# Logit matmuls in batches of eight, four logit banks, smaller PSUM and staging pools, and half-1 products written into the first phase

## The chip, the cores and the metric

The kernel runs on one core of a Trainium2 chip. The metric is device time in microseconds (us) of that core, taken over several executions; lower is better. A run here is slow when it lies over 1.5% above the fastest run of its kernel. The granted clock is the share of TensorE's full clock that the profile records. Engines are named as the profile names them: PE is TensorE (matmul), PEld its weight loads, DVE VectorE, ACT ScalarE, POOL GpSimd, SP SyncE (here it only issues DMAs). "L527" is line 527 of the kernel. "Compiled order" is the order in which the compiler puts the instructions on each engine; it can be read from a build, without a chip, and it isn't always the order of the source.

## The reference

Two independent blocks whose outputs are joined along the last axis. Part A is a dilated sliding-window attention (16 heads of 28, 8 taps, dilation 2); part B is a diagonal complex state-space layer ("S5").

```python
# A: x [1,2048,448] bf16
q, k, v = split(x @ wqkv)                       # 16 heads, Dh = 28
idx = pos[:, None] - 2 * arange(8)[None, :]     # W = 8 taps, dilation 2
logits = einsum("bhsd,bhswd->bhsw", q, k[idx]) * Dh**-0.5   # masked where idx < 0
o = einsum("bhsw,bhswd->bhsd", softmax(logits), v[idx])
a = o.reshape(B, S, D) @ wo
# B: h_t = Lam_bar * h_{t-1} + B_bar x_t ;  y = 2 Re(C h) + x * Dskip
out = concatenate([a, b], axis=-1)              # [1,2048,896] bf16
```

## The kernel before

Part B's recurrence (the "S5 chain") runs on VectorE. Its output needs 16 "y tiles": 12 matmuls of 128x448 each into one PSUM bank, a ScalarE cast into a staging buffer `yb`, and a store.

Part A's logits are made in two halves of the sequence. For every tap w and quarter mt of the heads, VectorE multiplies q by the shifted k (the tile `pr`, 32 of them a half, 64 in all), and TensorE sums over the head dimension with an indicator matrix into the logit banks `lg`, two banks a half, one per chunk `ci` of 512 columns. Softmax works on chunk after chunk of 512. After it come 56 products `td` of attention and gathered v, reductions of them into a PSUM bank `ot`, its eviction `oT`, and 16 output-projection tiles that use the same staging buffers `yb`. The core, with cuts marked:

```python
    ps_mm = pool("ps_mm", bufs=3, space=PSUM)     # projections, softmax      (shortened)
    ps_lg = pool("ps_lg", bufs=2, space=PSUM)     # logits: one half at a time
    ps_y  = pool("ps_y",  bufs=2, space=PSUM)
    ps_ot = pool("ps_ot", bufs=1, space=PSUM)
    ap: bufs=6 (pr)      yo: bufs=3 (yb)
    # ...
            p0 = A.products(0)
            for tl in range(HB // 128):
                B.y_slice(1, tl)                  # ... 12 matmuls, then:
                #   yb = yo.tile(...); nc.scalar.copy(yb[:], ps[:])
                #   nc.sync.dma_start(outv[...], yb[:])
                for em in p0[4 * tl:4 * tl + 4]:
                    em()
    # ... products(hf), one em per (w, mt):
                    pr = ap_.tile([112, HF], BF16, name="pr")
                    nc.vector.tensor_tensor(pr[:], qT[...], kT[...], op=ALU.mult)
                    for ci in range(HF // CH):
                        nc.tensor.matmul(lg[ci][32 * g:32 * g + 32, :], lhsT=IndZ[:, o0:o0 + 32],
                                         rhs=pr[:, ci * CH:(ci + 1) * CH], ...,
                                         tile_position=(0, 32 * g))      # g = w // 2
    # ... late():
            for gi in range(4):
                load_vwg(gi)                      # gathered v (vwG), 2 MB each, on SyncE's queue
            p1 = products(1)
            sm01 = zip_stages(softmax(0), softmax(1))
            left = interleave(sm01, p1, 3)        # 3 products after each softmax stage
```

## Time and profile before

| | before |
|---|---|
| median of 4 runs (range) | 284.79 us (284.36 to 285.24) |
| profiled span | 283.5 us |
| VectorE / TensorE busy | 75% / 71% |

The windows of before follow. A line is one stretch of time (from:to, its length), then busy us of each engine with the number of instructions, then the granted TensorE clock as a share of full speed, the DMA share and GB/s.

```profile
core 0: us, PE busy (x) PEld busy (x) DVE busy (x) ACT busy (x) POOL busy (x), PEclk, DMA share, GB/s
146.50:166.00 19.50, 19.30 (x66) 3.43 (x66) 19.50 (x33) 0.00 (x0) 0.00 (x0) 0.87 0.36 119
166.80:193.20 26.40, 25.21 (x133) 12.78 (x132) 1.98 (x5) 5.89 (x12) 0.00 (x0) 1.00 0.79 280
...
243.60:262.60 19.00, 12.60 (x66) 2.23 (x65) 19.00 (x32) 5.27 (x9) 0.00 (x0) 0.50 0.56 212
...
262.60:283.50 20.90, 17.27 (x70) 5.93 (x70) 0.01 (x1) 9.75 (x19) 0.00 (x0) 0.88 0.27 88
```

Four stages can be read there. From 146 VectorE is full with products and TensorE keeps up. From 167 TensorE is full with y tiles and VectorE almost empty. The last 19 us of the td products have a full VectorE and TensorE at half clock. In the tail VectorE has ended and TensorE works at the output projection.

VectorE's timeline around the y stage (start, duration, instruction group, and in brackets the idle time ahead of it and what ended it):

```profile
start us, us, engine line op out<-in xcount [idle before <-releaser]
...
145.76 22.97 DVE L527 TENSOR_TENSOR pr<-qT,kT 112x1024 bf16<-112x1024 bf16 x38
193.15 1.28 DVE L584 TENSOR_TENSOR m<-lg,t 64x512 f32<-64x512 f32 x2 [24.42 <-ACT t L580]
```

So 38 products run without a gap, 0.604 us each, and then VectorE waits 24.4 us for the softmax's first copy, which stands behind the y tiles.

From the waits (engine, line, what it waited for: us in total, times, longest):

```profile
...
DVE m L584 <- ACT t L580: 24.4, 1, 24.4
...
PE ot L637 <- ACT oT L642: 8.0, 9, 2.5
...
ACT yb L407 <- DMA out_dram<-yb: 6.9, 2, 4.5
```

The first line is the wait of the timeline again. The second is TensorE waiting nine times for its one `ot` bank to be evicted (copied out to SBUF). The third is a cast that waits for a staging buffer, because the store of its old content hasn't landed.

ScalarE in the tail of before:

```profile
start us, us, engine line op out<-in xcount [idle before <-releaser]
...
276.38 0.58 ACT L642 CAST oT<-ot 64x512 bf16<-64x512 f32 x1 [0.93 <-PE ot L637]
276.86 1.13 ACT L655 CAST yb<-y 128x448 bf16<-128x448 f32 x2
278.44 0.53 ACT L655 CAST yb<-y 128x448 bf16<-128x448 f32 x1 [0.45 <-PE y L652]
279.19 0.53 ACT L655 CAST yb<-y 128x448 bf16<-128x448 f32 x1 [0.23 <-PE y L652]
280.02 0.53 ACT L655 CAST yb<-y 128x448 bf16<-128x448 f32 x1 [0.29 <-PE y L652]
```

The last casts come singly, some 0.8 us apart, as TensorE finishes its tiles.

### The profile page before, as it was taken

The page shows a single profiled execution, that of the slowest core. Times are in us where ns is not written, and L with a number is a line of the kernel's source. Part 1 is how long each engine was busy: PE and PEld are TensorE (multiplying, and loading weights), DVE is VectorE, ACT ScalarE, POOL GpSimd, SP SyncE. Part 2 cuts the span into 40 slices and gives each one's busy share as a digit, 9 for nine tenths or more (in the row PEclk, how much of TensorE's full clock was granted, in tenths as well). Part 3 has the DMA queues.
Part 4 walks back from the last instruction along what each step waited for, and adds up shares of the span by engine and source line. Part 5 has one row for each costly group of instructions (what it writes and reads, how often), then busy time and mean ns, then how long its engine had stood idle before and what let it go on. Part 6 is the DMA issues. An engine that isn't in the chain of part 4 may idle for free.

```text
span 283.5 us, 2644 instructions
## 1 busy us (share of the span) xinstructions
PE 201.1 (71%) x836; PEld 76.5 (27%) x836; DVE 213.6 (75%) x324; ACT 126.2 (44%) x199; POOL 32.3 (11%) x58
## 2 busy tenths in 40 slices
PE   0067164298969896959539999986986635666994
PEld 0012032044535453525201135541211101111231
DVE  4907999989999999999999980005899629999000
ACT  4019319399675877466500002217603490222454
POOL 8928143000040000000000000002000000000000
PEclk9997759589988999999958999998799555555699
DMA  5999821113279998850027008992000005980132
GB/s 125 215 194 232 219 65 31 49 51 98 66 239 335 321 322 323 322 230 32 1 50 279 0 2 291 354 333 89 2 1 0 0 0 168 415 299 7 49 118 92
DMA packets 40109, 42.68 MB, mean 151 GB/s; under 512 B 26140, under 2 KB 32480, under 8 KB 40096
## 3 DMA queue, kind: packets, MB, share of 16 engines
q1 hardware_dynamic: 37984, 35.18, 40.3%
q0 software_dynamic: 2112, 7.34, 7.7%
q8 instruction: 6, 0.10, 0.1%
q14 instruction: 7, 0.06, 0.1%
HBM read 30.97 MB, written 20.20 MB: 180 GB/s over the span
## 4 chain that ended last, share of the span: by engine, by line
DVE 53%; PE 23%; DMA 7%; ACT 7%; issue 6%; SPq 4%; POOL 0%; DVEq 0%; ACTq 0%; POOLq 0%
PE lg L534 7%; DVE gre L378 6%; DVE gim L379 6%; DVE td L627 6%; DMA out_dram<-yb 5%; PE y L652 5%; PE ot L637 5%; DVE pr L527 4%; DVE wt L318 3%; DVE wt L320 2%; SPq L84 2%; DVE vre L365 2%; DVE tA L366 2%; DVE vre L367 2%; DVE tB L371 2%
## 5 line engine op out<-in xcount | busy, mean ns | idle before, releaser
L457 PE MATMUL mm<-xT_a,wq 128*112 128x512 bf16 x192 | 47.1, 401 | 14.9 <-DMA wq<-in_A_wqkv_dram 8.3
L344 PE MATMUL mm<-xT_b,wT_B 128*128 128x512 bf16 x128 | 34.5, 420 | 17.9 <-DMA wT_B<-in_B_B_re_dram 11.5
L534 PE MATMUL lg<-pr,IndZ 112*32 112x512 bf16 x128 | 35.9, 445 | 9.8 <-DVE pr L527 9.5
L527 DVE TENSOR_TENSOR pr<-qT,kT 112x1024 bf16<-112x1024 bf16 x64 | 38.9, 684 | 2.1 <-PE lg L534 2.1
L457 PEld LDWEIGHTS <-wq 128*112 128x112 bf16 x192 | 26.4, 138 | 34.9 <-issue 11.7
L627 DVE TENSOR_TENSOR td<-attnT,vwG 128x1024 bf16<-128x1024 bf16 x56 | 34.3, 681 | 0.0
L637 PE MATMUL ot<-td,FdZ 128*32 128x512 bf16 x112 | 23.4, 588 | 14.9 <-ACT oT L642 8.0
L398 PE MATMUL y<-Wt,hrh 128*128 128x448 bf16 x64 | 23.1, 361 | 10.4 <-DVE Wt L289 9.2
L407 ACT CAST yb<-y 128x448 bf16<-128x448 f32 x16 | 8.3, 535 | 47.7 <-PE y L404 40.8
L346 ACT CAST U<-mm 128x512 bf16<-128x512 f32 (+1 forms) x32 | 17.7, 582 | 17.5 <-PE mm L344 17.2
L344 PEld LDWEIGHTS <-wT_B 128*128 128x128 bf16 x128 | 13.3, 106 | 37.9 <-issue 12.8
L401 PE MATMUL y<-Wt,hih 128*128 128x448 bf16 x64 | 23.2, 362 | 0.1
L584 DVE TENSOR_TENSOR m<-lg,t 64x512 f32<-64x512 f32 x4 | 2.6, 677 | 24.4 <-ACT t L580 24.4
L642 ACT CAST oT<-ot 128x512 bf16<-128x512 f32 (+1 forms) x16 | 9.3, 583 | 24.9 <-PE ot L637 24.9
L652 PE MATMUL y<-wo_sb,oT 128*128 128x448 bf16 x64 | 17.6, 408 | 0.8 <-issue 0.7
L318 DVE SCALAR_TENSOR_TENSOR wt<-kint,cs,it 128x1024 f32<-128x1024 int32 (+1 forms) x8 | 10.2, 1279 | 8.9 <-ACT aw L325 8.9
L534 PEld LDWEIGHTS <-IndZ 112*32 112x32 bf16 x128 | 6.4, 97 | 38.4 <-issue 38.4
L404 PE MATMUL y<-Dg,xT_b 128*128 128x448 bf16 x64 | 14.9, 352 | 0.0
L465 ACT CAST vb<-mm 112x512 bf16<-112x512 f32 x16 | 9.1, 586 | 13.1 <-PE mm L457 12.7
L571 POOL MEMSET oT<- 64x2048 bf16 x1 | 1.8, 1800 | 111.6 <-PE y L404 111.6
L637 PEld LDWEIGHTS <-FdZ 128*32 128x32 bf16 x112 | 4.5, 104 | 35.5 <-issue 31.8
L323 ACT ACTIVATE S<-wt,cs 128x1024 bf16<-128x1024 f32 (+1 forms) x8 | 9.2, 1149 | 8.4 <-DVE wt L320 8.4
(134 smaller groups left out, 288.1 us busy)
## 6 DMA issues: line engine op xcount, KB each, us to landing
vwG<-vscr SPq DMA_DIRECT2D x7, 2048.0 KB, 9.4
vscr<-vscr SPq DMA_DIRECT2D x4, 1792.0 KB
vscr<-vscr POOLq DMA_DIRECT2D x4, 1792.0 KB, 36.4
out_dram<-yb SPq DMA_DIRECT2D x32, 112.0 KB, 1.9
vscr<-vb SPq DMA_DIRECT2D x16, 112.0 KB, 1.9
wq<-in_A_wqkv_dram SPq DMA_DIRECT2D x1, 1008.0 KB
wo_sb<-in_A_wo_dram SPq DMA_DIRECT2D x28, 14.0 KB, 1.8
wq<-in_A_wqkv_dram SPq DMA_DIRECT2D x1, 168.0 KB
```

What stands on the lines that cost most here:

```text
L318: nc.vector.scalar_tensor_tensor(wt[psl], in0=kint[psl], scalar=self.negTp[psl, j:j + 1], in1=it[psl, lo:lo + HB], op0=ALU.mult, op1=ALU.add)
L344: nc.tensor.matmul(ps[:, :], lhsT=self.BT[:, k, comp, c0:c0 + 128], rhs=self.xk(k, lo + ci * CH, CH), start=(k == 0), stop=(k == 3))
L346: nc.scalar.copy(Uc[psl, ci * CH:(ci + 1) * CH], ps[psl, :])
L378: nc.vector.tensor_tensor_scan(gre[psl], rb, vre[psl], i0, op0=ALU.mult, op1=ALU.add)
L398: nc.tensor.matmul(ps[:], lhsT=hrh[:, j, tl * 128:(tl + 1) * 128], rhs=self.Wt[:, j, 0, :], start=(n == 0), stop=False)
L401: nc.tensor.matmul(ps[:], lhsT=hih[:, j, tl * 128:(tl + 1) * 128], rhs=self.Wt[:, j, 1, :], start=False, stop=False)
L457: nc.tensor.matmul(ps[:112, :], lhsT=wq[:, k, f0:f0 + 112], rhs=self.xk(k, c * CH, CH), start=(k == 0), stop=(k == 3))
L527: nc.vector.tensor_tensor(pr[:], qT[:, mt, lo:lo + HF], kT[:, mt, lo - DIL * w: lo - DIL * w + HF], op=ALU.mult)
L534: nc.tensor.matmul(lg[ci][32 * g:32 * g + 32, :], lhsT=IndZ[:, o0:o0 + 32], rhs=pr[:, ci * CH:(ci + 1) * CH], start=first, stop=(lastq and ...
L627: nc.vector.tensor_tensor(td[:], attnT[:, hf * HF:(hf + 1) * HF], vw[:, hf * HF:(hf + 1) * HF], op=ALU.mult)
L637: nc.tensor.matmul(po[32 * q:32 * q + 32, :], lhsT=FdZ[:, o0:o0 + 32], rhs=tds[(d2, hf)][:, ci * CH:(ci + 1) * CH], start=(d2 % 2 == 0), s ...
L652: nc.tensor.matmul(ps[:], lhsT=oT[:, g, tt * 128:(tt + 1) * 128], rhs=wo_sb[:, g, :], start=(g == 0), stop=(g == 3))
```

## The change

The intent: all four logit banks live at once, so that half-1 products can be made under the y tiles, where VectorE idles; and the logit matmuls of four column groups stand together in batches of eight, so that they can overlap on TensorE. To make room, the PSUM pool of `ot` is merged into `mm` (now two buffers for both), and while `pr` grows by two tiles in SBUF, the staging buffers `yb` and the buffers `vb` (they hold the v projection on its way to DRAM) go from three to two.

```diff
-    ps_mm = ctx.enter_context(tc.tile_pool(name="ps_mm", bufs=3, space=PSUM))
-    ps_lg = ctx.enter_context(tc.tile_pool(name="ps_lg", bufs=2, space=PSUM))
+    ps_mm = ctx.enter_context(tc.tile_pool(name="ps_mm", bufs=2, space=PSUM))
+    ps_lg = ctx.enter_context(tc.tile_pool(name="ps_lg", bufs=4, space=PSUM))
...
-    ps_ot = ctx.enter_context(tc.tile_pool(name="ps_ot", bufs=1, space=PSUM))
+    ps_ot = ps_mm
...
-    pools["ap"] = ctx.enter_context(tc.tile_pool(name="ap", bufs=6))
-    pools["yo"] = ctx.enter_context(tc.tile_pool(name="yo", bufs=3))
+    pools["ap"] = ctx.enter_context(tc.tile_pool(name="ap", bufs=8))
+    pools["yo"] = ctx.enter_context(tc.tile_pool(name="yo", bufs=2))
...
-            p0 = A.products(0)
+            pg = A.products(0) + A.products(1)
+            A.p1_left = pg[14:]
             for tl in range(HB // 128):
                 B.y_slice(1, tl)
-                for em in p0[4 * tl:4 * tl + 4]:
+                for em in pg[:14][2 * tl:2 * tl + 2]:
                     em()
... (vb buffers: 3 -> 2)
... (products: one em per (par, mt) instead of per (w, mt))
+                    prs = []
+                    for g in range(4):
+                        w = 2 * g + par
+                        pr = ap_.tile([112, HF], BF16, name="pr")
+                        nc.vector.tensor_tensor(pr[:], qT[...], kT[...], op=ALU.mult)
+                        prs.append(pr)
                     for ci in range(HF // CH):
-                        nc.tensor.matmul(lg[ci][32 * g:32 * g + 32, :], ..., rhs=pr[:, ...], ...)
+                        for g in range(4):
+                            nc.tensor.matmul(lg[ci][32 * g:32 * g + 32, :], ..., rhs=prs[g][:, ...], ...)
...
-                                    po = ps_ot.tile([128, CH], F32, name="ot")
+                                    po = ps_ot.tile([128, CH], F32, name="mm")
...
-            p1 = products(1)
+                p1 = self.p1_left
             sm01 = zip_stages(softmax(0), softmax(1))
-            left = interleave(sm01, p1, 3)
+            left = interleave(sm01, p1, 1)
```

More of the change, by code (lines that the diff above doesn't have):

```diff
@@ L463, in proj_one @@
         else:
-            vb = self.pools["apj"].tile([112, CH], BF16, name=f"vb{(mt * NCH + c) % 3}")
+            vb = self.pools["apj"].tile([112, CH], BF16, name=f"vb{(mt * NCH + c) % 2}")
             nc.scalar.copy(vb[:], ps[:112, :])
@@ L519, in products @@
         self.lgs[hf] = lg
-        n = [0]
-        order = [(w, mt) for par in range(2) for mt in range(4) for w in range(par, W, 2)]
-        for (w, mt) in order:
-            if True:
-                def em(w=w, mt=mt):
-                    pr = ap_.tile([112, HF], BF16, name="pr")
-                    lo = PADL + hf * HF
-                    nc.vector.tensor_tensor(pr[:], qT[:, mt, lo:lo + HF],
-                                            kT[:, mt, lo - DIL * w: lo - DIL * w + HF], op=ALU.mult)
-                    g = w // 2
-                    o0 = 128 - (16 * (w % 2) + 4 * mt)
-                    first = (w % 2 == 0 and mt == 0)
-                    lastq = (w % 2 == 1 and mt == 3)
-                    for ci in range(HF // CH):
-                        nc.tensor.matmul(lg[ci][32 * g:32 * g + 32, :], lhsT=IndZ[:, o0:o0 + 32],
-                                         rhs=pr[:, ci * CH:(ci + 1) * CH],
-                                         start=first, stop=(lastq and not (hf == 0 and ci == 0)),
-                                         tile_position=(0, 32 * g))
-                    n[0] += 1
+        lo = PADL + hf * HF
@@ new lines, in products, with em @@
+        for par in range(2):
+            for mt in range(4):
+                def em(par=par, mt=mt):
+                    prs = []
+                    for g in range(4):
+                        w = 2 * g + par
+                        pr = ap_.tile([112, HF], BF16, name="pr")
+                        nc.vector.tensor_tensor(pr[:], qT[:, mt, lo:lo + HF],
+                                                kT[:, mt, lo - DIL * w: lo - DIL * w + HF], op=ALU.mult)
+                        prs.append(pr)
+                    o0 = 128 - (16 * par + 4 * mt)
+                    first = (par == 0 and mt == 0)
+                    lastq = (par == 1 and mt == 3)
+                    for ci in range(HF // CH):
+                        for g in range(4):
+                            nc.tensor.matmul(lg[ci][32 * g:32 * g + 32, :], lhsT=IndZ[:, o0:o0 + 32],
+                                             rhs=prs[g][:, ci * CH:(ci + 1) * CH],
+                                             start=first, stop=(lastq and not (hf == 0 and ci == 0)),
+                                             tile_position=(0, 32 * g))
@@ L539, in em @@
                     if hf == 0 and lastq:
-                        nc.tensor.matmul(lg[0][32 * g:32 * g + 32, :], lhsT=MaskL[:, 32 * g:32 * g + 32],
-                                         rhs=MaskR[:], start=False, stop=True, tile_position=(0, 32 * g))
+                        for g in range(4):
+                            nc.tensor.matmul(lg[0][32 * g:32 * g + 32, :], lhsT=MaskL[:, 32 * g:32 * g + 32],
+                                             rhs=MaskR[:], start=False, stop=True, tile_position=(0, 32 * g))
@@ L673, in late @@
             if 0 not in lgs:
-                for em in products(0):
-                    em()
-            p1 = products(1)
+                p1 = products(0) + products(1)
+            else:
+                p1 = self.p1_left
             sm01 = zip_stages(softmax(0), softmax(1))
-            left = interleave(sm01, p1, 3)
+            left = interleave(sm01, p1, 1)
             for em in left:
```

## The prediction

> **What bounds the kernel now.** The span is 283.5 us. Windows and engine timelines of before show its stages.
> (a) 23 to 146 us: VectorE is full (26.8 of 27 us busy at 119-146); the S5 chain bounds it.
> (b) 146 to 167: half-0 products, one per 0.604 us on VectorE (38 in 22.97 us); TensorE reduces each as it comes, clock 0.75 to 1.00.
> (c) 167 to 193: 11 y tiles on TensorE at 2.27 us each. VectorE runs 6 half-1 products ahead, then is idle 24.4 us, the longest wait listed.
> (d) 193 to 216: softmax of chunks 0 and 1, hidden under 26 half-1 products.
> (e) 216 to 234: softmax of chunks 2 and 3, with 8 td products in its gaps.
> (f) 234 to 262.6: 48 td products. (g) a 20.9 us tail: output projection and stores.
>
> **What the change does.** No arithmetic goes or comes. Logit matmuls come in batches of 8 over four column groups; all four logit banks live at once; mm has 2 PSUM buffers (shared with ot) instead of 3; output staging 2 instead of 3, vb 2 instead of 3, pr 8 instead of 6.
>
> Decisive is the compiled order. The intent is products under y tiles, but TensorE's order after is: all 128 logit matmuls, then 12 y tiles, then all softmax matmuls. VectorE's order is 64 products, then softmax. The Trainium skill ("TensorE: Matmul & The Clock Gate", Part 2) says matmuls stay in program order; the trace of before agrees, its order being the compiled one. So the y tiles wait for 64 products instead of 32, VectorE still idles under them, and the softmax loses the products that hid it.
>
> **Costs, all on the critical path:**
> - y tiles start after 64 products instead of 32: 32 x 0.604 = +19.3 us.
> - y stage: one tile more, +2.3. The batched logits leave TensorE mostly idle, so its clock should fall (same page, Part 1; before shows 0.50 in the td stage, with matmuls in bursts): +1.5. Two staging buffers wait for stores behind the 2 MB vwG loads (stores took 6.8 and 8.3 us there in the chain of waits): +1.5. Stage about 30 us instead of 26.4.
> - From the last y tile to the last attention tile: before 41 us. After, no products in it: two softmax rounds, about 21 us of ScalarE work (7 table loads of 1.28 us, 12 activations near 0.6, 8 copies), plus one wait behind 7 td products: estimated 26. -15.
> - Tail: a store lands 1.9 us after issue, plus a 0.53 us cast; with two buffers a tile takes about 1.3 us, against 0.8 to 1.05 for TensorE now: +3.
> - Stage (a): more waits for vb stores and 2 PSUM buffers, mostly in slack: +1.
> Batching saves nothing: VectorE sets the pace there.
>
> Sum: 19.3 + 5.3 - 15 + 3 + 1 = +13; I shade it to +11. **Predicted 296 us, range 289 to 302.** Chances: faster by over 2% 0.03, within 2% 0.11, slower 0.86.
>
> **Right if the profile after shows:** 62 products in an unbroken VectorE run of about 38 us from 146; TensorE under half clock there; y tiles from about 186 to 216; VectorE nearly idle some 30 us; two softmax rounds for about 26 us; last td near 271; casts in the tail waiting for stores.
>
> **Wrong if:** stage (a) slips by over 3 us (U casts late); softmax rounds are much shorter or overlap the y tiles; stores free their buffers faster than 1.9 us, so that the tail doesn't grow; or matmul batches slow VectorE.

## The result, and the profile after

| | before | after |
|---|---|---|
| median of all runs (range) | 284.32 us (282.5 to 285.24), 16 runs | 289.82 us (288.49 to 292.73), 11 runs |
| ratio of fast runs [95%] | 1 | 1.0207 [1.0177, 1.0237] |
| profiled span | 283.5 us | 287.9 us |

A ratio here, as in all experiments, is the mean time of one kernel's fast runs over that of the other's of the same rounds, so it isn't quite the ratio of the medians quoted beside it. The change costs about 2%, some 5.5 us; the interval spans the 2% line. The prediction said +11.

The windows of after, for the stages that answer to those shown of before:

```profile
core 0: us, PE busy (x) PEld busy (x) DVE busy (x) ACT busy (x) POOL busy (x), PEclk, DMA share, GB/s
146.50:166.00 19.50, 18.45 (x68) 3.15 (x68) 19.47 (x33) 0.00 (x0) 0.00 (x0) 0.83 0.61 227
...
184.80:215.20 30.40, 27.80 (x145) 13.99 (x144) 0.14 (x1) 6.42 (x13) 0.00 (x0) 1.00 0.50 180
...
248.40:267.40 19.00, 12.90 (x68) 3.24 (x67) 18.97 (x32) 6.26 (x12) 0.00 (x0) 1.00 0.56 213
...
267.40:287.90 20.50, 12.41 (x62) 5.47 (x60) 0.00 (x0) 7.90 (x17) 0.00 (x0) 0.96 0.27 90
```

Two things stand out. The y tiles now come at 185 to 215 with VectorE empty: the idle stretch has moved, not gone. And in the last 19 us of the td products the clock is 1.00 instead of 0.50, with TensorE's busy time nearly the same (12.9 against 12.6 us). The tail then has 62 matmuls left instead of 70, yet takes as long.

VectorE's timeline, and the waits, of after:

```profile
start us, us, engine line op out<-in xcount [idle before <-releaser]
...
146.87 37.42 DVE L529 TENSOR_TENSOR pr<-qT,kT 112x1024 bf16<-112x1024 bf16 x62
215.06 1.28 DVE L587 TENSOR_TENSOR m<-lg,t 64x512 f32<-64x512 f32 x2 [30.78 <-ACT t L583]
```

```profile
...
DVE m L587 <- ACT t L583: 30.8, 1, 30.8
...
ACT yb L408 <- DMA out_dram<-yb: 9.7, 2, 4.9
...
PE mm L640 <- ACT oT L645: 2.1, 5, 0.5
```

All 64 products (two of them inside the S5 chain, 62 in one run of 37.4 us) come ahead of the y tiles, and VectorE then waits 30.8 us. Waits for a free staging buffer grew from 6.9 to 9.7 us. TensorE's wait for an `ot` eviction (8.0 us before) is 2.1 us in five waits; the tile is named mm there.

ScalarE and TensorE in the tail of after:

```profile
start us, us, engine line op out<-in xcount [idle before <-releaser]
...
274.56 0.98 ACT L658 CAST yb<-y 128x448 bf16<-128x448 f32 x2 [1.37 <-PE y L655]
276.92 0.97 ACT L658 CAST yb<-y 128x448 bf16<-128x448 f32 x2 [1.38 <-PE y L655]
```

```profile
start us, us, engine line op out<-in xcount [idle before <-releaser]
...
272.79 1.67 PE L655 MATMUL y<-wo_sb,oT 128*128 128x448 bf16 x8 [0.68 <-ACT yb L658]
275.14 1.67 PE L655 MATMUL y<-wo_sb,oT 128*128 128x448 bf16 x8 [0.68 <-ACT yb L658]
```

Casts come in pairs every 2.35 us, two tiles at a time, so 1.18 us a tile. The profile puts their wait down to TensorE. But the first tile of a pair has had its four matmuls done halfway through the 1.67 us, and its cast still starts together with the second. What it waits for by the times is the store: a cast (0.53) and the store after it (issue to landing 1.7 us for all ten in this stretch) make 2.2 of the 2.35 us. The Trainium skill ("DMA: Bandwidth & Descriptors", the table "Two cost components") gives a fixed cost of about 2.0 us, fitted for DMAs issued from GpSimd; these 112 KB stores are issued from SyncE and took 1.7 us, so they don't test that figure.

The ledger, from the two profiles:

| step | before, us | after, us | difference | predicted |
|---|---|---|---|---|
| S5 chain ends | 145.7 | 146.8, with two products (1.2) inside | 0 | +1 |
| first y tile behind the logits starts | 166.76 | 184.86 | +18.1 | +19.3 |
| from there to the softmax's first copy | 25.8 | 29.6 | +3.8 | +5.3 |
| from that copy to the last attention chunk | 41.1 | 23.9 | -17.2 | -15 |
| 48 td products | 29.0 | 29.0 | 0 | 0 |
| tail | 20.9 | 20.6 | -0.3 | +3 |
| sum | | | +4.4 | +13 (shaded to +11) |

The sum agrees with the difference of the spans (4.4 us). Twelve y tiles stand behind the logits in after, eleven in before. The swap of order, +18.1 and -17.2, nearly cancels in this ledger.

Builds show two parts of the change that had no effect. A build of the changed kernel with the pull taken out of the source, four logit banks left, has the same instructions in the same order on every engine: the banks let VectorE run ahead, the source order does not (it wasn't run). And past the first batch the compiled order of TensorE has the logit matmuls in pairs again, one product's ci 0 and ci 1, as before. The trace agrees: these are starts of logit matmuls in each kernel, in us.

```
before: 150.121  150.501  150.725  151.103
after:  150.018  150.398  150.620  150.998  151.221
```

Both alternate gaps of about 0.38 and 0.22 us. No batch of eight is to be seen.

### The profile page after: what moved, and what is told of

It reads as the page before. It is cut to its first block, busy times and chain, and to the rows that moved or that the text cites. A ratio compares the mean times of both kernels' runs of the same rounds, so it can differ in the third digit from the quotient of the medians.

```text
span 287.9 us, 2649 instructions
## 1 busy us (share of the span) xinstructions
PE 199.4 (69%) x836; PEld 76.6 (27%) x836; DVE 213.9 (74%) x324; ACT 126.3 (44%) x199; POOL 32.0 (11%) x58
## 4 chain that ended last, share of the span: by engine, by line
DVE 33%; PE 25%; ACT 6%; DMA 4%; issue 3%; ACTq 0%; DVEq 0%
PE lg L537 13%; DVE td L630 8%; PE y L655 4%; DMA out_dram<-yb 4%; DVE gre L379 4%; DVE gim L380 4%; PE y L399 2%; PE y L405 2%; PE y L402 2%; ACT yb L658 1%; DVE wt L319 1%; PE mm L640 1%; DVE tA L367 1%; DVE hih L389 1%; DVE vre L368 1%
## 5 line engine op out<-in xcount | busy, mean ns | idle before, releaser
L458 PE MATMUL mm<-xT_a,wq 128*112 128x512 bf16 x192 | 48.4, 402 | 15.4 <-DMA wq<-in_A_wqkv_dram 6.1
L345 PE MATMUL mm<-xT_b,wT_B 128*128 128x512 bf16 x128 | 34.1, 417 | 16.1 <-DMA wT_B<-in_B_B_re_dram 11.7
L537 PE MATMUL lg<-pr,IndZ 112*32 112x512 bf16 x128 | 37.5, 415 | 7.0 <-DVE pr L529 6.5
L347 ACT CAST U<-mm 128x512 bf16<-128x512 f32 (+1 forms) x32 | 18.3, 583 | 21.7 <-PE mm L345 21.6
L640 PE MATMUL mm<-td,FdZ 128*32 128x512 bf16 x112 | 21.9, 450 | 7.8 <-DVE td L630 5.1
L587 DVE TENSOR_TENSOR m<-lg,t 64x512 f32<-64x512 f32 x4 | 2.6, 678 | 30.9 <-ACT t L583 30.8
L645 ACT CAST oT<-mm 128x512 bf16<-128x512 f32 (+1 forms) x16 | 8.7, 586 | 23.4 <-PE mm L640 23.4
L655 PE MATMUL y<-wo_sb,oT 128*128 128x448 bf16 x64 | 14.3, 358 | 5.9 <-ACT yb L658 4.1
L402 PEld LDWEIGHTS <-hih 128*128 128x128 bf16 x64 | 6.3, 99 | 22.0 <-issue 15.5
```

The source lines that it names most:

```text
L345: nc.tensor.matmul(ps[:, :], lhsT=self.BT[:, k, comp, c0:c0 + 128], rhs=self.xk(k, lo + ci * CH, CH), start=(k == 0), stop=(k == 3))
L347: nc.scalar.copy(Uc[psl, ci * CH:(ci + 1) * CH], ps[psl, :])
L402: nc.tensor.matmul(ps[:], lhsT=hih[:, j, tl * 128:(tl + 1) * 128], rhs=self.Wt[:, j, 1, :], start=False, stop=False)
L458: nc.tensor.matmul(ps[:112, :], lhsT=wq[:, k, f0:f0 + 112], rhs=self.xk(k, c * CH, CH), start=(k == 0), stop=(k == 3))
L640: nc.tensor.matmul(po[32 * q:32 * q + 32, :], lhsT=FdZ[:, o0:o0 + 32], rhs=tds[(d2, hf)][:, ci * CH:(ci + 1) * CH], start=(d2 % 2 == 0), s ...
L655: nc.tensor.matmul(ps[:], lhsT=oT[:, g, tt * 128:(tt + 1) * 128], rhs=wo_sb[:, g, :], start=(g == 0), stop=(g == 3))
```

## The experiments

Theory ORDER says that the loss comes from the order swap that four logit banks cause (the prediction's view). STAGING says that it comes from the cut of `yb` from three buffers to two. A third matter is the second PSUM bank for `ot`, which the prediction left out. All twelve kernels gave correct results. Medians below are of four runs, beside before's 283.63, 284.41 and 283.77 us in the three groups e1 to e4, e5 to e8 and e9 to e12.

### e1: the changed kernel with two logit banks

```diff
-    ps_lg = ...bufs=4        +    ps_lg = ...bufs=2
-    pg = A.products(0) + A.products(1); A.p1_left = pg[14:]
+    pg = A.products(0)       # one batch after each y tile; p1 = products(1) later
```

> The changed kernel with two logit banks (one half) instead of four, half-1 products made in the softmax stage as before; batches, 2 mm buffers, 2 staging buffers, 2 vb buffers, 8 pr buffers as in the changed kernel. Theory ORDER (the fourth bank lets all 64 products and 128 logit matmuls go ahead of the y tiles, +18 us to their start, and strips the softmax of its cover): y tiles start near 167 us again and the time returns to 284 to 287 us. Rival SQUEEZE (the smaller PSUM and staging pools cost the time): stays at 288 to 291 us.

Measured: 286.33 us, ratio 1.0116 [1.0086, 1.0146]. The order is before's again: y tiles from 165 (twelve of them, as in after), last attention chunk at 234.8 instead of 238.4 us. The time lies in the range that ORDER expected. So going back on the order swap gives 0.9%, some 2.6 us. It isn't the loss by itself: the kernel is still slower than before, with a tail of 20.6 us like after's.

### e2: before with four logit banks, mm and ot sharing two

```diff
-    ps_mm bufs=3, ps_lg bufs=2, ps_ot bufs=1
+    ps_mm bufs=2, ps_lg bufs=4, ps_ot = ps_mm     # nothing else
```

> The kernel before with only the PSUM split of the change (4 logit banks, 2 mm buffers shared with ot); no batches, 3 staging buffers, 3 vb, 6 pr. ORDER: y tiles start near 185 us, first attention tile after them, time 286 to 290 us, i.e. most of the loss without any batching or pulling in the source. SQUEEZE by staging buffers: near 284 us, since staging is as before.

Measured: 278.98 us, ratio 0.9851 [0.9824, 0.9879]. This kernel has the swap in full (logits end at 182.9, softmax starts at 208.4 us) and is faster than before, so neither expectation held. That the swap alone makes the kernel slower than before falls here. The gain sits in the td stage and the tail, 16.1 us instead of 20.9:

```profile
core 0: us, PE busy (x) PEld busy (x) DVE busy (x) ACT busy (x) POOL busy (x), PEclk, DMA share, GB/s
242.20:261.20 19.00, 12.87 (x68) 3.17 (x67) 19.00 (x32) 6.20 (x12) 0.00 (x0) 1.00 0.57 214
261.20:277.30 16.10, 12.29 (x62) 5.35 (x60) 0.04 (x1) 8.48 (x17) 0.00 (x0) 1.00 0.35 114
```

### e3: before with batches only

```diff
     # pools as before; products() as in the change; interleave(sm01, p1, 1)
```

> The kernel before with only the batched emission of logit matmuls (8 per batch over four column groups). The compiled order still has the matmuls in pairs as their product comes, so ORDER expects no change: 282.5 to 286 us, and granted clock in the product stage as before (0.88). Rival BATCHING COUNTS: 1 per cent or more away from before, with a lower clock in the product stage.

Measured: 282.84 us, ratio 1.0005 [0.9963, 1.0047]. Batching in the source is worth nothing here. But the trace has the matmuls one product at a time again, with starts 0.22 and 0.38 us apart, so real batches aren't tested before e8 and e9. The `ot` bank is single, and so the clock at the end of the td products is 0.50 and the tail 21.0 us.

### e4: the changed kernel with y stores on ScalarE's queue

```diff
-        nc.sync.dma_start(self.outv[...448:896], yb[:])
+        nc.scalar.dma_start(self.outv[...448:896], yb[:])
```

> The changed kernel with one edit: the y tiles' stores are issued from ScalarE's queue instead of SyncE's. The compiled order of TensorE then has the last y tiles between the logit matmuls. ORDER: y tiles run under the products, VectorE's idle stretch of 31 us shrinks to under 18, time 264 to 276 us. If it is TensorE that bounds the mixed stage (12 y tiles x 2.27 + 128 x 0.215 = 55 us from about 144) the y tiles end near 198 instead of 215: 270 us. SQUEEZE: within 2 us of 290.

Measured: 273.04 us, ratio 0.9639 [0.9612, 0.9667]. The edit does more than move a store: the compiler now interleaves y tiles and logit matmuls, so y tiles end at 189 and products at 196.3 us, and the last attention chunk is done at 217.3 instead of 238.4. In after the y stores stand behind the 2 MB vwG loads on SyncE's queue, where two of them took 7.05 and 5.09 us to land instead of 1.7. The Trainium skill ("DMA: Bandwidth & Descriptors", section "Queues, rings and completion order") says that SyncE and ScalarE each own one queue row, with rings on the same 16 DMA engines, where descriptors are consumed in ring order. A queue of their own did not make the stores quick: issued at 162.94 and 173.28 us, beside vwG loads in flight, two of them still took 6.34 and 5.94 us in e4, and one issued at 168.43 took 1.67. The waits for a staging buffer did fall, from 9.7 to 1.7 us. How much of the gain is the order and how much the stores, this run alone doesn't tell.

### e5: the changed kernel with three staging buffers

```diff
-    yo bufs=2                +    yo bufs=3
-    FdZ [128, 240]           +    FdZ [128, 144]    # unused columns; makes room in SBUF
```

> The changed kernel with 3 output staging buffers instead of 2 (room made by trimming an unused part of a constant; vb stays at 2, mm at 2, four logit banks and batches stay). New theory STAGING (the change loses by the two staging buffers: 12th y tile and stalls in the y stage +3.8 us, projection tail +4.4 us against the run with four banks only; without that it gains): y stage 26.5 us, tail near 16 us, time 280 to 283 us. Rival SQUEEZE BY mm OR vb: 286 us or more.

Measured: 280.49 us, ratio 0.988 [0.9843, 0.9916]: the changed kernel gains 3.3% (1.0207 against 0.988) from one buffer. The stage from logits to softmax takes 25.9 us instead of 29.6 (the compiler puts the twelfth y tile back ahead of the logits), and the tail 16.1 instead of 20.6. ScalarE in its tail:

```profile
start us, us, engine line op out<-in xcount [idle before <-releaser]
...
272.96 0.53 ACT L658 CAST yb<-y 128x448 bf16<-128x448 f32 x1 [0.29 <-PE y L655]
273.75 0.53 ACT L658 CAST yb<-y 128x448 bf16<-128x448 f32 x1 [0.26 <-PE y L655]
274.54 0.53 ACT L658 CAST yb<-y 128x448 bf16<-128x448 f32 x1 [0.26 <-PE y L655]
```

Single casts 0.79 us apart, in place of after's pairs every 2.35. STAGING is confirmed, and so is the reading of after's tail above.

### e6: before with two staging buffers

```diff
-    yo bufs=3                +    yo bufs=2
```

> The kernel before with 2 staging buffers instead of 3, nothing else. STAGING: the y stage has 12 tiles and stalls (30 us instead of 26.4), the tail grows by 0 to 3 us (there TensorE's half clock hides part): 286.5 to 290.5 us. Rival: within 1 us of before.

Measured: 293.1 us, ratio 1.0311 [1.0261, 1.036], slower than expected. The softmax starts 3.6 us later than in before (196.1 against 192.5), and the tail takes 27.5 us against 20.9. The single `ot` bank and the two staging buffers add up in the tail, where the lost buffer costs 6.5 us here and 4.5 between e5 and after. The clock is 0.50 ahead of it,

```profile
core 0: us, PE busy (x) PEld busy (x) DVE busy (x) ACT busy (x) POOL busy (x), PEclk, DMA share, GB/s
247.40:266.40 19.00, 12.60 (x66) 2.29 (x65) 18.95 (x32) 5.27 (x9) 0.00 (x0) 0.50 0.52 209
266.40:293.80 27.40, 18.85 (x70) 6.54 (x70) 0.00 (x0) 9.25 (x19) 0.00 (x0) 0.81 0.20 67
```

and 70 matmuls are left for it, as in before.

### e7: before with mm and ot sharing four banks

```diff
-    ps_mm bufs=3, ps_ot bufs=1     +    ps_mm bufs=4, ps_ot = ps_mm
```

> The kernel before with the output reduction (ot) drawn from the mm pool of 4 banks instead of its own single bank; two logit banks, 3 staging buffers. Theory CLOCK (a second bank for ot lets TensorE run its td-stage matmuls densely enough to leave half clock, so that the tail starts warm): granted clock in the td stage goes from 0.50 to near 1.00 and the tail from 20.9 to about 16 us: 278 to 281 us. Rival (the warm clock comes from the four logit banks or the order of the softmax): clock stays 0.50, 282.5 us or more.

Measured: 277.59 us, ratio 0.9788 [0.9743, 0.9833], just under the expected range. The number of PSUM banks is the same; they are only pooled, so that two `ot` tiles can be alive.

```profile
core 0: us, PE busy (x) PEld busy (x) DVE busy (x) ACT busy (x) POOL busy (x), PEclk, DMA share, GB/s
242.80:261.80 19.00, 13.64 (x68) 3.25 (x67) 18.98 (x32) 6.25 (x12) 0.00 (x0) 1.00 0.53 211
261.80:277.80 16.00, 12.18 (x62) 5.27 (x59) 0.00 (x0) 8.44 (x17) 0.00 (x0) 0.97 0.35 115
```

With e2, e3, e5 and e6 this fills the table of the tail (from the last td product to the end, us):

| | three staging buffers | two staging buffers |
|---|---|---|
| one ot bank | 20.9 (before), 21.0 (e3) | 27.5 (e6) |
| ot sharing mm | 16.0 (e7), 16.1 (e2), 16.1 (e5) | 20.6 (e1), 20.6 (after) |

Without exception the runs of the first row have a granted clock of 0.50 in the last 19 us of the td products, and those of the second row 1.00. The later runs, which all share the banks, agree: clock 1.00, and a tail of 16.1 us with three buffers (e11, e12) and of 20.6 with two (e4, e8, e9).

### e8: the changed kernel with TensorE's order forced, and ScalarE stores

```diff
+            with tc.manual_schedule(engines={mybir.EngineType.PE}):
                 for tl in range(HB // 128):
                     B.y_slice(1, tl)
                     for em in pg[:14][2 * tl:2 * tl + 2]:
                         em()
     # and y stores on nc.scalar, as in e4
```

> The changed kernel with y stores on ScalarE's queue and TensorE's order forced to the written one in the product loop: y tile, two batches of 8 logit matmuls, and so on. The batches then really stand together. If four column groups run side by side, 128 logit matmuls cost TensorE about 8 to 12 us instead of 27, and products, not TensorE, bound the mixed stage: VectorE's 62 products in 38 to 41 us, y end near 187, time 260 to 267 us. If batching is worth nothing, within 2 us of the run with the store queue alone (273).

Measured: 264.35 us, ratio 0.9315 [0.9271, 0.9359]. Here the intent of the change is carried out as written: y tiles end at 187 and products at 188.8 us, side by side. VectorE's only wait within the stage is one behind the first y tiles:

```profile
start us, us, engine line op out<-in xcount [idle before <-releaser]
...
146.49 3.70 DVE L530 TENSOR_TENSOR pr<-qT,kT 112x1024 bf16<-112x1024 bf16 x6
155.04 33.80 DVE L530 TENSOR_TENSOR pr<-qT,kT 112x1024 bf16<-112x1024 bf16 x56 [4.86 <-PE lg L538]
```

In whole batches the logit matmuls of different column groups do run together: starts from the trace, in us, four and four:

```
154.328 154.331 154.334 154.338   154.554 154.557 154.560 154.564
```

### e9: as e8, with pairs in place of batches

```diff
-                    for ci in range(HF // CH):
-                        for g in range(4):
+                        for ci in range(HF // CH):       # inside the loop over g
```

> As the forced-order run (264.4 us), but the 8 logit matmuls of a batch stand in pairs of one product and one column group, as the compiler places them in the changed kernel. Theory BATCHES PAY ONLY WHERE TENSORE BOUNDS: a pair is two matmuls one after the other on one column group, so 128 cost TensorE about 27 us instead of 8 to 12, and the mixed stage becomes TensorE's: y end 197 to 203 instead of 187, 272 to 278 us. Rival: pairs of different column groups overlap anyway: within 2 us of 264.4.

Measured: 264.62 us, ratio 0.9328 [0.9307, 0.9349]. The loss of the overlap that I had expected did not come; the rival held. Neighbouring pairs belong to different column groups and overlap too, with starts 6 to 7 ns apart in its trace where the products are ready. A build of e9 shows that TensorE's order there is ci 0, ci 1 of one column group, then ci 0, ci 1 of the next. The trace has it otherwise: the four ci 0 start at 152.634 to 152.654 us and the four ci 1 at 152.860 to 152.880 (told apart by the semaphore that only a pair's second matmul increments). So the statement cited in the prediction, that matmuls stay in program order, does not hold between column groups here; the coarse order, on which the prediction rests, is as compiled. The gain of e8 over e4 is thus the coarse order, not the batch. Of its 9 us I can argue one part: each change from a full-width y matmul to a column-group logit matmul or back costs about 0.1 us. In e4's trace a y matmul is followed by a logit matmul after 0.283 us and by another y matmul after 0.189; a logit matmul by a y matmul after 0.31 and by one of its kind in the same column group after 0.215. The Trainium skill ("TensorEngine Tiling (Array Packing)", section "Key Properties") says that a change of tiling mode drains TensorE; the trace agrees. e4 mostly changes every one to four matmuls, 57 times in all, e8 every twelve to sixteen, 15 times. An estimate from these counts is 42 changes of 0.1 us, about 4 of the 9 us; the rest is not explained.

### e10: the changed kernel with sixteen whole batches forced ahead of the y tiles

```diff
+            with tc.manual_schedule(engines={mybir.EngineType.PE}):
+                for em in pg:
+                    em()
+                A.p1_left = []
+                for tl in range(HB // 128):
+                    B.y_slice(1, tl)
```

> The changed kernel with TensorE's order forced to 16 whole batches, then the y tiles (stores as in the changed kernel). Tests a step of the prediction that the compiled order had made void: batches leave TensorE mostly idle, so its granted clock falls. If so: clock in the product stage 0.5 to 0.7 instead of 0.83 to 1.00, first y tiles slow, 290 to 292 us. Rival: short bursts every 2.4 us keep the clock at 0.83 or more: 288 to 290 us.

Measured: 291.56 us (291.41 for the three fast runs), ratio 1.0258 [1.0231, 1.0285]; the runs were 296.1, 290.55, 291.71 and 291.41. This tests the prediction's step that batches leave TensorE idle and lower its clock. The time is where it was expected, a little above after's 289.82. The profile, though, fell in the run of 296.1 us, which counts as slow. It shows 0.50 of the clock from 146.5 to 190, where after shows 0.83 and 1.00; how much of that belongs to the batches and how much to the slow run I can't tell. But the mean clock over the whole span is, for the fast runs, 0.841 to 0.847 in e10's three, 0.887 to 0.911 in after's. So the forced batches do come with a lower clock in fast runs; where in the span it fell is shown by the slow profile alone.

### e11: as e8, batches ahead of their y tile, three staging buffers

```diff
-    yo bufs=2, FdZ [128, 240]     +    yo bufs=3, FdZ [128, 144]
-                    B.y_slice(1, tl)
                     for em in pg[:14][2 * tl:2 * tl + 2]:
                         em()
+                    B.y_slice(1, tl)
```

> As the forced-order run with 3 staging buffers and each y tile after its two batches instead of before. It should take away the 4.9 us for which VectorE waits in the forced-order run behind three y tiles, partly, and shorten the tail by about 3 us: 257 to 261 us.

Measured: 261.07 us, ratio 0.92 [0.9177, 0.9223], a hair outside the range. The last attention chunk is done at 209.3 us.

### e12: as e11, one batch per y tile, half-1 products left for the softmax

```diff
-                    for em in pg[:14][2 * tl:2 * tl + 2]:
-                        em()
+                    pg[tl]()
                     B.y_slice(1, tl)
+            A.p1_left = pg[8:]
```

> As e11, but the y tiles stand between the 8 half-0 batches, and the half-1 batches come after them, so that the softmax of chunks 0 and 1 again runs under half-1 products. y end near 172 to 176, last attention tile near 197 to 203 instead of 210, 250 to 256 us. If the softmax chunks wait on something else than the y tiles' buffers: within 2 us of e11.

Measured: 259.97 us, ratio 0.9155 [0.9128, 0.9181]. By its median it is the fastest kernel here (its interval touches e11's), but it missed the expected 250 to 256. The y tiles end at 175 as hoped, yet the last attention chunk is done only at 208.6 us. ScalarE shows why:

```profile
start us, us, engine line op out<-in xcount [idle before <-releaser]
...
176.85 1.28 ACT L606 ACT_TABLE_LOAD   x1
187.85 0.60 ACT L606 ACTIVATE e<-lg 128x512 bf16<-128x512 f32 x1 [9.71 <-PE lg L603]
```

The exponential waits 9.7 us for a matmul which needs `negm` (the negated maximum of the softmax), and VectorE's timeline has `negm` of the first two chunks only at 186.70 and 189.71, behind half-1 products. The products hide the softmax's work but delay its links on VectorE.

## Why the prediction was right or wrong

The range held, and slower was the right direction. The point, 296, was 6 us too high, and the text put its weight on the wrong step. That the range held was in part luck: 289.82 lies 0.8 us above its lower end, and most of the loss came from the staging buffers, while a gain of 4.9 us was not foreseen.

- **"Decisive is the compiled order."** The order was read rightly: 62 products in one run of 37.4 us, y tiles at 185 to 215, VectorE idle for 30.8 us. As the main cause of the loss the step failed by its size. The prediction's two terms net to +4.3 us. In the ledger the swap costs +18.1 us at the start of the y tiles and gives -17.2 back in the softmax, which was itself lengthened before by the products in it. e1 against after puts the swap at 0.9% (2.6 us), e7 against e2 at 0.6%, where mm's buffers differ too and the intervals overlap.
- **"Tail ... +3"** failed, by an omitted term. The mechanism named, casts that wait for stores, is there, at 1.18 us a tile for 1.3 predicted, and costs 4.5 us (e5's 16.1 against after's 20.6). But the second bank for `ot`, visible in the diff and left without a cost, gives 4.9 us back (before's 20.9 against e7's 16.0). Net -0.3.
- **"Clock should fall: +1.5"** failed in the y stage and in the products ahead of it (1.00, and 0.83 against before's 0.87). The compiler had undone the batches that were to leave TensorE idle. The step had nothing to act on. e10, which forces the batches, speaks for it: its fast runs have a lower mean clock (0.841 to 0.847 against 0.887 to 0.911) and a median 1.6 us above after's, but the intervals of the two ratios overlap, and that the clock makes this difference is not shown.
- **y stage, +5.3** came out at +3.8; without the void clock term it is 3.8. One tile more (+2.3) and staging stalls (+1.5) were right in their sum, and e5 shows that both go with the staging cut: its stage is 25.9 us.
- **Softmax, -15** came out at -17.2, **stage (a), +1** at 0, **y start, +19.3** at +18.1: terms a little off, all in the same direction. Of the 9.2 us between the predicted terms (13.6 before shading) and the measured 4.4, these three make 4.4, the tail 3.3 and the clock 1.5.
- **"Batching saves nothing"** holds: in the source by e3, and for real batches against pairs by e9.

Where the time went can be told as a chain of kernels, by their ratios to before: with `ot` sharing mm's banks 0.979 (e7), with four logit banks at two mm buffers 0.985 (e2), with batches, `pr` 8 and `vb` 2 as well 0.988 (e5; the intervals of e2 and e5 overlap), with two staging buffers 1.021 (after). The one buffer taken from staging costs 3.3%, and hides the 2.1% that the pooled `ot` bank brings. The intended gain, products under y tiles, never took place in after, because the compiled order didn't follow the source; e4, e8 and e12 show that it is there to be had.

What stays open: why the second `ot` bank brings the clock from 0.50 to 1.00. Waits on the eviction go away with it (8.0 us to 2.1), and the Trainium skill ("TensorE: Matmul & The Clock Gate", section "A second HAM failure mode: psum-queue depth-cycling") describes short idles from cycling through PSUM that lower the clock. All fourteen profiles, three with one `ot` bank and eleven with shared banks, agree without exception; but the idles themselves weren't varied apart from the bank. Open too is more than half of the 9 us between e4 and e8, and how e4's gain divides between order and stores.

## What to carry to other kernels

Cost every line of a diff that shrinks or merges a buffer pool, not only the lines that the change is about: here a staging buffer cost 3.3% and a merged PSUM pool brought 2.1%, and the headline moves were worth under 1%. Staging buffers are too few when cast plus store landing, divided by the number of buffers, exceeds the time of one tile on the engine that feeds it (here 2.35 us over two, 1.18, against 0.8; over three it would be 0.78). And look in the compiled order whether an interleaving written in the source is still there; if not, the experiment that forces it shows what the idea is worth.

## What the Trainium skill lacked or had wrong

- "TensorE: Matmul & The Clock Gate", psum-queue depth-cycling: the page speaks of a clock that goes back and forth. Here it was 0.50 over a whole stretch of 19 us with TensorE busy 66% of it (12.6 us), and 1.00 at 68% (12.9 us) once two banks could cycle. The section doesn't say that a second PSUM buffer can lift this.
- "TensorEngine Tiling (Array Packing)", Key Properties: the drain at a change of tiling mode has no number. Between full-width and column-group matmuls it was about 0.1 us each way (0.283 against 0.189 us, and 0.31 against 0.215).
- "DMA: Bandwidth & Descriptors": the page has no time from issue to landing for a small store from SyncE or ScalarE. A 112 KB store landed 1.7 us after its issue when it was undisturbed, and after 5.1 to 7.1 us with 2 MB loads in flight on its own queue (after), or 5.9 and 6.3 us with them on the other queue (e4). Nor does it draw the consequence for the number of staging buffers.
- No page read warns that a tile scheduler can undo both an interleaving and a batching written in the source: a build without the pull has the same instructions as the one with it, and matmul starts stayed 0.22 and 0.38 us apart.
